# Keys and queries of the last two row blocks as seven products of half matrices, with the mixing drawn into the same block

## The chip, the cores and the metric

The kernel runs on one core of a Trainium2 chip. The metric is the device time of one execution in microseconds (us). Five engines work side by side, each on its own list of instructions in order: TensorE (PE) multiplies matrices into banks of PSUM, VectorE (DVE) and ScalarE (ACT) work element by element and can read PSUM, GpSimd (POOL) does small work and issues transfers that add to their target, and SyncE (SP) issues all other transfers (DMA).

## The reference

`x` has 2048 rows of 512 numbers. Everything is float32.

```python
xn = _layernorm(x)
# A: linear attention, 32 heads of 16
q, k, v = heads(xn2 @ wqkv)                # xn2: xn, 512 x 1536 weights
phi = lambda t: jnp.where(t > 0, t + 1, jnp.exp(t)) + 1e-6
kv = einsum("bhsd,bhse->bhde", phi(k), v); z = phi(k) summed over rows
s = ((phi(q) @ kv) / (phi(q) . z + 1e-6)) @ wo
# B: mixer
h = gelu(_layernorm(xn) @ w1)              # 512 x 512
hs = (four column groups of h, shifted by +1, -1, +2, -2 rows) @ w2
x1 = xn + hs
g = silu(x1 + gelu(_layernorm(x1) @ w3) @ w4)   # 512 x 1376 x 512
return x + s * g
```

Here `xn2` is `xn` (the block A is called with it), and `heads` cuts the columns into q, k and v.

## The kernel before, in words

**Precision.** TensorE multiplies in the rounded type float32r. Each operand is cut into a high and a low part (`rounded`, L478: ACT copies to float32r, DVE subtracts), and each product is three matmuls: high by high, high by low, low by high (`products`, L470). A product over 512 columns of weights with the four chunks of 128 that make up 512 is 12 matmuls of 128x512.

**Work.** The 16 row tiles of 128 rows form four blocks of four (block b holds tiles 4b to 4b+3). `XT` is x turned, loaded by `load_u` (L635); its parts are `UT`, with two columns at either side for the shifts (`split_halo`, L658). Per tile, `key` (L752) and `query` (L765) each run 12 matmuls against `WK` or `WQ`. The mean of a row is taken out afterwards: DVE computes `ps - mean * (column sums of the weights)` in one operation, on `wneg` and `qneg` (`feature_k`, L739, and `query`). Then ACT makes relu and exp, scaled by the row's inverse deviation `rs1`. The key's feature goes to `gram` (L776), 12 matmuls that gather features times normalized rows in the four PSUM banks `acc`; its sum over rows is gathered by an adding transfer on POOL (`zacc`). The query's feature goes to memory (`pqd`, by SP and, adding, by POOL).

`mixer` (L873) multiplies by `W1` (48 matmuls of 512 columns per block, `mix1`), applies the gelu, and makes the forms for the product with `W2`. That product is done by seven products of half matrices in place of eight (`seven`, L783: Winograd's form; the sums of quarters are `s1` to `s4` on one side and `t1` to `t4` on the other, `right`, L806). `mix2(i)` (L882) runs it for tiles i and i+2, in 42 matmuls of 256 columns; three PSUM banks (`pa`, `pb`, `pe`) are used in turn, and ACT and DVE take partial results out between products. An adding transfer puts the normalized rows to it. Half-way, the gathered matrix is multiplied by `wv` and `wo` (`kv`, `m`).

The second half runs block after block over W3 and W4 (`up_pair`, `down`, again by sevens) and the attention's product (`attend_pair`), and ends with `gate`. `make_pair` (L942) loads and cuts a pair of columns of W3; `AHEAD` (L425) says how many microseconds ahead of need its buffers may be taken.

**Order.** The functions only add operations to a plan. `Plan.emit` (L267) then simulates the engines at build time with fixed costs and puts the operations in order: PE's follow the order in which they were added, except that later ones may go ahead inside a window of 12 us; each other operation has a due time, worked back from the matmul that needs it (`deadlines`, `backward`). SBUF is a fixed number of buffers (`counts`, L431: 90 pieces "p" of 516 numbers per partition); a buffer is handed out no earlier than `lead` microseconds ahead of the due time. `SOONER` (L1401) is a table of operation numbers and quarter microseconds by which their due time is moved. PSUM is handed out as four banks "acc" and four "mm".

The order around the change is written in the loop over b = 1, 2, 3 behind the opening: it loads block b and runs its keys and queries between pieces of earlier blocks' mixing: blocks 0 and 1 are mixed in the pass for block 2, block 2 in the pass for block 3, and the last block behind the loop.

Of the kernel before, what the change touches and what calls it, by code (L numbers as in the profile page):

```python
# [12 lines left out]
AX = mybir.AxisListType  # L13

P = 128
EPS = 1e-5
DEN_EPS = 1e-6
TINY = 1e-6
# [67 lines left out]
class Plan:  # L86
# [180 lines left out]
    def emit(self, first, lead, reserve, window, ahead, table=()):  # L267
# [20 lines left out]
        while left:  # L288
# [105 lines left out]
def linear_attn_gated_by_mixer(  # L394
# [20 lines left out]
    QT = 4  # L415
# [18 lines left out]
    for tag, n in counts.items():  # L434
# [62 lines left out]
    arow = memory("arow", S + 2 * EDGE, 1)  # L497

    def pool(busy, reads, out, fn):
        pl.add("POOL", busy, busy, reads, [out], fn)  # L500
# [112 lines left out]

    ABC = {}

    def spread_a(b):

        ps = pl.new("mm", f"ab{b}", F32, 512)[:QT, :P]
        pl.transpose(ps, au[:, b * QT:(b + 1) * QT], ident.all)
        t = pl.new("p", f"ar{b}", F32, PIECE)[:QT, :P]  # L620
        pl.act(t, ps, AF.Copy)
        row = arow[:, EDGE + b * BT:EDGE + (b + 1) * BT]
        pl.store(row.via(lambda ap: ap.rearrange("o (j p) -> (o j) p", p=P)), t)

    def join_a(b):

# [8 lines left out]
    def load_u(b, parts):  # L635

        n = BT // parts
        UT[b] = [[pl.new("p", f"u{b}_{c}{k}", F32R, PIECE) for k in "hl"] for c in range(NC)]
        for q in range(parts):
            o = q * n  # L640
            for c in range(NC):
                if q == 0:
                    XT[b, c] = piece(f"xt{b}_{c}")
                if c and parts > 1:
                    if q == 0:
                        pl.load(XT[b, c], xt[b, c])
# [3 lines left out]
                pl.load(src, xt[b, c][:, o:o + n])  # L650
                hi, lo = (t[:, 2 + o:2 + o + n] for t in UT[b][c])
                if b == q == 0 and parts > 1:
                    pl.ts(hi, src, 1.0, None, ALU.mult)
                    split(lo, src, hi)
                else:
                    rounded(hi, lo, src)

    def split_halo(b):  # L658
        for c in range(NC):
# [102 lines left out]

    pqd = {i: memory(f"pqd{i}") for i in range(NT)}

    def query(i):  # L765
        ps = bank(f"q{i}")
        project(ps, i, WQ, range(NC))
        t, e, r = (piece(f"q{n}{i}") for n in "ter")
        pl.stt(t, qneg, mean(mv1, i), ps, ALU.mult, ALU.add)
# [4 lines left out]
        pl.soon(pl.gather(pqd[i].all, e))  # L774

    def gram(i):  # L776
        xh, xl, kh, kl = GK.pop(i)
# [437 lines left out]
    WQ = Weights("wq", wqkv[0])  # L1215
    WQ.split()
    sums(WQ, bank("qsum"), qneg)
    query(0)
    gram(0)
    query(1)  # L1220
    load_u(1, 1)
    load_rows(QT)
    scale_x(QT, 1)
    gram(1)
    query(2)
    gram(2)
    query(3)
    gram(3)
    key(QT)
    pl.load(hal.all, halo.rearrange("p q c -> p (q c)"))  # L1230
    scale_u(0)
    spread_a(0)
    W1 = Weights("w1", w1)
    early_s, early_f = EARLY
    fill = [lambda f=f: make_w4(f) for f in early_f] + [lambda s=s: make_pair(s) for s in early_s]
    for b in range(1, NQ):
        t0 = b * QT

        def more(n):
            if b > 1:  # L1240
                for _ in range(n):
                    if fill:
                        fill.pop(0)()

        for j in range(b == 1, QT):
            load_rows(t0 + j)
        split_halo(b - 1)
        scale_x(t0 + (b == 1), QT - (b == 1))
        scale_u(b)
        if b == 2:  # L1250
            pl.early = 20.0
            prepare_w2()
            pl.early = 0.0
            mixer(0)
        if b > 1:
            load_u(b, 1)
            key(t0)
        if b == 2:
            mix2(0)
        query(t0)  # L1260
        if b == 2:
            mix2(1)
        spread_a(b)
        more(2)
        if b > 1:
            mixer(b - 1)
        key(t0 + 1)
        query(t0 + 1)
        more(2)
        gram(t0)  # L1270
        key(t0 + 2)
        if b > 1:
            mix2(t0 - QT)
        else:
            W1.center(by_dma=True)
            W1.split()
        query(t0 + 2)
        more(2)
        gram(t0 + 1)
        key(t0 + 3)  # L1280
        if b > 1:
            mix2(t0 - QT + 1)
        query(t0 + 3)
        more(2)
        if b < NQ - 1:
            gram(t0 + 2)
            gram(t0 + 3)


    b = NQ - 1  # L1290
    split_halo(b)
    mixer(b)
    gram(NT - 2)
    gram(NT - 1)
# [39 lines left out]
    for b in range(NQ):  # L1334
# [64 lines left out]
                gate(b * QT + QT - 1, a, o, D // 2, late=True, by_dma=False, whole=o > 0)  # L1399

    SOONER = (  # L1401
# [6 lines left out]
    )  # L1408
    pl.emit(first=6.0, lead={"p": 14.0, "w": 14.0, "ab": 10.0}, reserve={"p": 20, "w": 1, "ab": 0}, window=12.0,
            ahead=6.0, table=SOONER)  # L1410
# [37 lines left out]
```

## Time and profile before

| | us |
|---|---|
| median of 3 runs | 519.35 (519.34 to 519.38) |
| span of the profiled execution | 517.6 |
| busy PE, DVE, ACT, POOL in it | 511.2, 394.0, 324.8, 102.8 |

The span runs from the first instruction to the last; the run's time has 1.7 us more around it. In a profile, an engine's busy share is the union of its instructions; matmuls overlap, so what one of them costs in a stream is the distance of two starts and not its duration. "L146" is a line of the kernel, mostly a helper's, so groups are told apart by the tiles that they write (`k`, `q`, `g`, `h`, `pb`).

### The profile page before, as it was taken

Reading aid. Unit: us, or ns where it says so; the run is one execution under the profiler, and the core shown is the slowest. Engines: PE = TensorE matmul, PEld = TensorE weight load, DVE = VectorE, ACT = ScalarE, POOL = GpSimd, SP = SyncE. Lnnn points to the kernel's source line nnn. Section 1 sums busy time; section 2 is a strip of 40 time slices with the busy share of each in tenths; the row PEclk is TensorE's granted clock in tenths of the full one; section 3 lists DMA queues with packets and bytes.
Section 4 is the critical chain, followed back from the end, with each engine's and each line's share of the span. In section 5 each row is a group of like instructions: output and inputs, shape, how many; then the busy total and the mean of one; then the engine's idle time right before and its main releaser. Section 6 shows DMA issues by size and latency. Waiting matters only on the chain.

```text
span 517.6 us, 8927 instructions
## 1 busy us (share of the span) xinstructions
PE 511.2 (99%) x3005; PEld 445.0 (86%) x3005; DVE 394.0 (76%) x788; ACT 324.8 (63%) x664; POOL 102.8 (20%) x195
## 2 busy tenths in 40 slices
PE   8999999999999999999999999999999999999996
PEld 6777888988888888898889989899898898999985
DVE  5884987569567838999999999655886657895635
ACT  5899784579558657787866755345453545535621
POOL 1378643431363022211100001000020000200000
PEclk9999999999999999999999999999999999999999
DMA  8759994375976389989767759648488376687604
GB/s 277 255 101 248 225 205 97 74 172 182 220 169 162 68 185 249 259 261 262 287 200 225 237 175 249 212 152 208 133 214 276 122 201 157 179 248 225 243 1 122
DMA packets 73281, 100.12 MB, mean 193 GB/s; under 512 B 7844, under 2 KB 30900, under 8 KB 73236
## 3 DMA queue, kind: packets, MB, share of 16 engines
q1 hardware_dynamic: 63876, 82.52, 50.6%
q0 software_dynamic: 9360, 17.04, 19.9%
q8 instruction: 23, 0.38, 0.3%
q14 instruction: 22, 0.18, 0.1%
HBM read 60.33 MB, written 30.81 MB: 176 GB/s over the span
## 4 chain that ended last, share of the span: by engine, by line
PE 91%; ACT 5%; DVE 2%; DMA 1%; issue 1%; SPq 0%; DVEq 0%
PE acc L146 22%; PE pb L146 10%; PE k L146 8%; PE h L146 8%; PE q L146 7%; PE g L146 7%; PE pe L146 5%; PE pbs L146 5%; PE pbm L146 4%; PE pa L146 3%; PE pes L146 2%; PE a L146 2%; PE pem L146 2%; PE pas L146 1%; ACT y L167 1%; PE pam L146 1%
## 5 line engine op out<-in xcount | busy, mean ns | idle before, releaser
L223 POOL DMA_DIRECT2D th<-in_x x14 | 12.2, 919 | 247.3 <-PE a L146 126.2
L167 ACT ACTIVATE p<-pb 128x256 f32<-128x256 f32 x20 | 7.7, 385 | 25.8 <-PE pb L146 25.4
L223 POOL DMA_DIRECT2D o<-x x16 | 15.0, 935 | 40.4 <-DVE o L189 19.7
L223 POOL DMA_DIRECT2D zacc<-kr x16 | 14.6, 910 | 41.8 <-DVE kr L199 33.6
L167 ACT ACTIVATE th<-xo 128x512 f32<-128x512 f32 (+1 forms) x16 | 9.7, 619 | 19.3 <-DVE xo L189 16.2
L167 ACT ACTIVATE gf<-gf 128x512 f32<-128x512 f32 (+1 forms) x40 | 20.9, 523 | 0.8
L223 POOL DMA_DIRECT2D pqd<-qe x16 | 14.7, 921 | 28.9 <-ACT p5m L167 10.0
L167 ACT ACTIVATE p<-pe 128x256 f32<-128x256 f32 x20 | 7.7, 386 | 18.9 <-PE pe L146 18.9
L189 DVE TENSOR_TENSOR xo<-acc,xo 128x512 f32<-128x512 f32 (+1 forms) x16 | 10.3, 670 | 11.4 <-PE acc L146 11.4
L199 DVE SCALAR_TENSOR_TENSOR kt<-wneg,mv,k 128x512 f32<-128x512 f32 x16 | 11.9, 742 | 9.4 <-PE k L146 8.5
L199 DVE SCALAR_TENSOR_TENSOR kr<-kt,kr 128x512 f32<-128x512 f32 x16 | 11.0, 690 | 10.4 <-ACT kt L167 10.4
L199 DVE SCALAR_TENSOR_TENSOR qt<-qneg,mv,q 128x512 f32<-128x512 f32 x16 | 11.9, 742 | 7.2 <-PE q L146 7.1
L167 ACT ACTIVATE ht<-ht 128x512 f32<-128x512 f32 x16 | 10.0, 630 | 11.5 <-DVE ht L189 11.4
L189 DVE TENSOR_TENSOR gf<-u,pe 128x256 f32<-128x256 f32 x20 | 8.3, 416 | 11.2 <-PE pe L146 11.2
L189 DVE TENSOR_TENSOR gf<-pa,p 128x256 f32<-128x256 f32 x20 | 8.4, 418 | 10.5 <-PE pa L146 10.4
L189 DVE TENSOR_TENSOR ht<-h,abc 128x512 f32<-128x512 f32 x16 | 10.8, 686 | 6.5 <-PE h L146 6.5
L167 ACT ACTIVATE x<-x,nm,rs 128x512 f32<-128x512 f32 x16 | 12.5, 802 | 2.9 <-POOL nm L189 2.9
L167 ACT ACTIVATE qr<-qt,rs 128x512 f32<-128x512 f32 x16 | 11.4, 715 | 4.1 <-DVE qt L199 4.1
L590 DVE BATCH_NORM_STATS2 st<-o 128x6 f32<-128x512 f32 x16 | 10.9, 683 | 1.8 <-DMA o<-x 1.8
L167 ACT ACTIVATE kr<-kt,rs 128x512 f32<-128x512 f32 x16 | 11.4, 715 | 1.2 <-DVE kt L199 1.1
L167 ACT ACTIVATE y<-o,nm,rs 128x512 f32<-128x512 f32 x16 | 12.0, 805 | 0.1
L167 ACT ACTIVATE kt<-kt,rs 128x512 f32<-128x512 f32 x16 | 11.4, 715 | 0.1
(1559 smaller groups left out, 2195.9 us busy)
## 6 DMA issues: line engine op xcount, KB each, us to landing
w_s<-in_w SPq DMA_DIRECT2D x28, 256.0 KB, 5.5
x<-in_x SPq DMA_DIRECT2D x16, 256.0 KB, 5.2
zacc<-kr POOLq DMA_DIRECT2D x16, 256.0 KB, 3.9
pqd<-qr SPq DMA_DIRECT2D x16, 256.0 KB, 3.3
pqd<-qe POOLq DMA_DIRECT2D x16, 256.0 KB, 5.4
o<-x POOLq DMA_DIRECT2D x16, 256.0 KB, 4.6
x1d<-o SPq DMA_DIRECT2D x16, 256.0 KB, 4.9
pq<-pqd SPq DMA_DIRECT2D x16, 256.0 KB, 6.0
```

The source lines that it names most:

```text
L146: lambda: nc.tensor.matmul(out.get(), lhs.get(), rhs.get(), start=start, stop=stop, skip_group_check=more))
L167: nc.scalar.activation(out.get(), src.get(), func, scale=get(scale), **kw)
L189: self.vec(eng, out, [a, b], lambda: self.e(eng).tensor_tensor(out.get(), a.get(), b.get(), op=op), True)
L199: lambda: self.nc.vector.scalar_tensor_tensor(out.get(), a.get(), get(s), b.get(), op0=op0, op1=op1),
L223: lambda: self.nc.gpsimd.dma_start(out.get(), get(src), accum_op=ALU.add), mb=mb)
L590: pl.add("DVE", .62, .69, [xv], [st], lambda: nc.vector.bn_stats(st.get(), xv.get()))
```

## The change

In blocks 2 and 3, keys and queries of a pair of tiles (i, i+2) come from one product by sevens: the turned rows are the left matrix, with its halves by rows (tiles 0, 1 against 2, 3 of the block) and by chunks (0, 1 against 2, 3), and the right matrix is [WK | WQ], with its halves by chunks and by weight. A product is 2 chunks x 3 matmuls of 512 columns. Keys and queries of tile i come out as `p1` and `u2`, those of tile i+2 as `pb` (left in PSUM) and `p5`.

For this the rows must be centred before they are multiplied: the means are turned into a row in memory (`spread_m`), spread over all partitions by a transfer, and subtracted from `XT` by DVE (`make_u`), which also makes the four sums of quarters (on POOL) and their parts. The correction by `wneg` and `qneg` falls away in these blocks. The forms of the two weights are made once (`forms_kq`). The rows of x of blocks 2 and 3 are loaded twice, once for their moments (`stats_of`) and later for the gram. The parts of `W1` are stored to memory after they are made and loaded again for blocks 2 and 3 (`w1_for`).

The loop gives way to a written order, in which the mixing of block 0 stands among the keys of block 1, that of block 1 behind them and before the keys of block 2, and those of blocks 2 and 3 among and behind the keys of their own block. The number of pieces goes from 90 to 96, `AHEAD` is longer, a buffer's lead is cut when few are free (`SCARCE`), the table `SOONER` is a new one, and the descriptor scratch of POOL's transfers is set to 4096 bytes. Blocks 0 and 1 keep their form (`KQ1 = False`).

```diff
+SCARCE = 3.0
...
                             n = lead[t.tag] * (1.5 if len(q) > reserve[t.tag] else 1)
+                            if t.tag == "p":
+                                n = min(n, SCARCE * (len(q) - need + 1))
...
+    SUMS = "POOL"
+    SOON = {"T": 24.0, "u": 5.0}
-    AHEAD = 30.0, 20.0, 10.0, 0.0, 0.0
+    AHEAD = 70.0, 50.0, 30.0, 10.0, 0.0
...
-    counts = {"w": 2, "p": 90, "h": 6, "sm": 12, "ab": 2, "acc": 4, "mm": 4}
+    counts = {"w": 2, "p": 96, "h": 6, "sm": 10, "ab": 2, "acc": 4, "mm": 4}
...
+    def make_u(b):
+        m = piece(f"um{b}")
+        pl.fetch(m, mrow[:, b * BT:(b + 1) * BT].via(lambda ap: ap.to_broadcast([P, BT])))
+        for c in range(NC):
+            pl.tt(XT[b, c], XT[b, c], m, ALU.subtract)
+            rounded(*(t[:, 2:2 + BT] for t in UT[b][c]), XT[b, c])
...
+        for n, u, v, op in ((0, q[1, 0], q[1, 1], ALU.add), (1, parts[0], q[0, 0], ALU.subtract),
+                            (2, q[0, 0], q[1, 0], ALU.subtract), (3, q[0, 1], parts[1], ALU.subtract)):
+            for c in range(2):
+                pl.tt(parts[n][c], u[c], v[c], op, eng=SUMS)
+            hl = rounds(f"us{b}_{n}")
+            rounded(*hl, s[n])
...
-    def feature_k(i, ps):
+    def feature_k(i, ps, centred=False):
         t, r = piece(f"kt{i}"), piece(f"kr{i}")
-        pl.stt(t, wneg, mean(mv1, i), ps, ALU.mult, ALU.add)
-        pl.act(r, t, AF.Relu, scale=col(rs1, i))
-        pl.act(t, t, AF.Exp, scale=col(rs1, i))
+        if not centred:
+            pl.stt(t, wneg, mean(mv1, i), ps, ALU.mult, ALU.add)
+            ps = t
+        pl.act(r, ps, AF.Relu, scale=col(rs1, i))
+        pl.act(t, ps, AF.Exp, scale=col(rs1, i))
...
+    def keys_queries(b, j):
+        i, k = b * QT + j, b * QT + j + 2
...
+        go(pb, "a11", "b11")
+        pl.act(p1, pb, AF.Copy)
+        go(pe, "s1", "t1")
+        pl.act(p5, pe, AF.Copy)
+        go(pb, "s2", "t2", False)
+        pl.act(u2, pb, AF.Copy)
+        go(pa, "a12", "b21")
+        pl.tt(p1, pa, p1, ALU.add)
+        go(pb, "s3", "t3", False)
+        pl.tt(p5, pb, p5, ALU.add)
+        go(pe, "s4", "b22", False)
+        pl.tt(u2, u2, pe, ALU.add)
+        feature_k(i, p1, True)
+        go(pb, "a22", "t4", False)
+        feature_k(k, pb, True)
+        feature_q(i, u2)
+        feature_q(k, p5)
...
+        ORD = [("q", 4), ("w1", 0), ("k", 5), ("g", 4), ("q", 5), ("st", 2), ("k", 6), ("g", 5), ("mix", 0), ("q", 6), ("w2",), ("k", 7), ("g", 6), ("T",), ("q", 7), ("g", 7)]
+    ORD += [("a", 2), ("h", 1), ("m2", 0), ("mix", 1), ("m2", 1), ("u", 2), ("m2", 4), ("m2", 5), ("x", 2),
+           ("kq", 2, 0), ("st", 3), ("g", 8), ("w1", 2), ("h", 2), ("a", 3), ("mix", 2), ("g", 10), ("kq", 2, 1), ("m2", 8), ("g", 9),
+           ("u", 3), ("m2", 9), ("g", 11), ("x", 3),
+           ("kq", 3, 0), ("g", 12), ("w1", 3), ("kq", 3, 1), ("g", 14)]
...
-    nc = bacc.Bacc("TRN2", target_bir_lowering=False, num_devices=1)
+    nc = bacc.Bacc("TRN2", target_bir_lowering=False, num_devices=1, dynamic_dma_scratch_size=4096)
```

In the written order "q", "k", "kq" and "g" are queries, keys, both by sevens and grams; "mix" and "m2" the two products of the mixing; "st", "x" and "u" the first load of the rows with their moments, the second load with the scaling, and `make_u`; "w1", "w2" and "T" the forms of W1, of W2 and of the two weights; "a" and "h" the row scales and the halo.

More of the change, by code (lines that the diff above doesn't have):

```diff
@@ L614, in linear_attn_gated_by_mixer, with spread, spread_m @@
     ABC = {}
-    def spread_a(b):
[L618 to L623, printed above, removed]
+    def spread(name, src, b, row):
+        ps = pl.new("mm", f"{name}b{b}", F32, 512)[:QT, :P]
+        pl.transpose(ps, src, ident.all)
+        t = pl.new("p", f"{name}r{b}", F32, PIECE)[:QT, :P]
+        pl.act(t, ps, AF.Copy)
+        pl.store(row.via(lambda ap: ap.rearrange("o (j p) -> (o j) p", p=P)), t)
+    def spread_a(b):
+        spread("a", au[:, b * QT:(b + 1) * QT], b, arow[:, EDGE + b * BT:EDGE + (b + 1) * BT])
+    def spread_m(b):
+        spread("c", means(mv1, b * QT, (b + 1) * QT), b, mrow[:, b * BT:(b + 1) * BT])
     def join_a(b):
@@ L763, in linear_attn_gated_by_mixer, with feature_q @@
     pqd = {i: memory(f"pqd{i}") for i in range(NT)}
[L765 to L769, printed above, removed]
+    def feature_q(i, t):
+        e, r = (piece(f"q{n}{i}") for n in "er")
         pl.act(by_block(e), by_chunk(t), AF.Relu, scale=col(ns1, i))
@@ L774, in query, with forms_kq, go @@
         pl.soon(pl.gather(pqd[i].all, e))
+    def query(i):
+        ps = bank(f"q{i}")
+        project(ps, i, WQ, range(NC))
+        t = piece(f"qt{i}")
+        pl.stt(t, qneg, mean(mv1, i), ps, ALU.mult, ALU.add)
+        feature_q(i, t)
+    TW = {}
+    def forms_kq():
+        k, q = WK.raw, WQ.raw
+        t = [[piece(f"kq{n}_{c}") for c in range(2)] for n in range(4)]
+        for c in range(2):
+            pl.tt(t[0][c], q[c], k[c], ALU.subtract)
+        for c in range(2):
+            pl.tt(t[1][c], q[c + 2], t[0][c], ALU.subtract)
+        for c in range(2):
+            pl.tt(t[2][c], q[c + 2], q[c], ALU.subtract)
+        for c in range(2):
+            pl.tt(t[3][c], k[c + 2], t[1][c], ALU.subtract)
+        for n in range(4):
+            TW[f"t{n + 1}"] = []
+            for c in range(2):
+                hl = rounds(f"kq{n}_{c}")
+                rounded(*hl, t[n][c])
+                TW[f"t{n + 1}"].append(hl)
+        TW["b11"], TW["b21"], TW["b22"] = WK.hl[:2], WK.hl[2:], WQ.hl[2:]
+    def keys_queries(b, j):
+        i, k = b * QT + j, b * QT + j + 2
+        pa, pb, pe = (bank(f"{n}k{i}") for n in ("pa", "pb", "pe"))
+        p1, p5, u2 = (piece(f"{n}k{i}") for n in ("p1", "p5", "u2"))
+        def go(ps, x, y, start=True):
+            products(ps, [both(U[b][x][c], j * P, (j + 1) * P) + TW[y][c] for c in range(2)], start, more=not start)
+        go(pb, "a11", "b11")
[15 more added lines that the diff above has]
+        feature_q(k, p5)
     def gram(i):
@@ L1221, in linear_attn_gated_by_mixer @@
     load_u(1, 1)
-    load_rows(QT)
-    scale_x(QT, 1)
+    if KQ1:
+        forms_kq()
+    scaled(1)
     gram(1)
+    if KQ1:
+        stats_of(1, False)
     query(2)
@@ L1227, in linear_attn_gated_by_mixer @@
     query(3)
+    if KQ1:
+        make_u(1)
     gram(3)
-    key(QT)
     pl.load(hal.all, halo.rearrange("p q c -> p (q c)"))
@@ L1232, in linear_attn_gated_by_mixer @@
     spread_a(0)
+    split_halo(0)
+    if not KQ1:
+        plain_u(1)
+        key(4)
+        scale_u(1)
+    spread_a(1)
     W1 = Weights("w1", w1)
@@ L1235, in linear_attn_gated_by_mixer @@
     fill = [lambda f=f: make_w4(f) for f in early_f] + [lambda s=s: make_pair(s) for s in early_s]
[L1236 to L1287, printed above, removed]
+    if KQ1:
+        ORD = [("kq", 1, 0), ("w1", 0), ("st", 2), ("g", 4), ("kq", 1, 1), ("g", 6), ("g", 5), ("mix", 0), ("w2",), ("g", 7)]
+    else:
+        ORD = [("q", 4), ("w1", 0), ("k", 5), ("g", 4), ("q", 5), ("st", 2), ("k", 6), ("g", 5), ("mix", 0), ("q", 6), ("w2",), ("k", 7), ("g", 6), ("T",), ("q", 7), ("g", 7)]
+    ORD += [("a", 2), ("h", 1), ("m2", 0), ("mix", 1), ("m2", 1), ("u", 2), ("m2", 4), ("m2", 5), ("x", 2),
[3 rows of a table added]
+    DO = {"x": scaled, "kq": keys_queries, "w1": w1_for, "st": stats_of, "g": gram, "mix": mixer, "w2": prepare_w2,
+          "a": spread_a, "h": split_halo, "m2": mix2, "u": make_u, "k": key, "q": query, "T": forms_kq}
+    for what, *args in ORD:
+        pl.early = SOON.get(what, 0.0)
+        DO[what](*args)
+    pl.early = 0.0
+    t0 = NT - QT
     b = NQ - 1
@@ L1292, in linear_attn_gated_by_mixer @@
     mixer(b)
-    gram(NT - 2)
-    gram(NT - 1)
+    gram(13)
+    gram(15)
     WV, WO = Weights("wv", wqkv[2]), Weights("wo", wo)
```

53 lines of the change are left out of this document (52 added, 1 removed), and 6 rows, old and new, of the table SOONER.

## The prediction

> **What bounds the kernel now.** I read the head of the page first: busy shares, then the 40 slices.
>
> ```profile
> span 517.6 us, 8927 instructions
> PE 511.2 (99%) x3005; PEld 445.0 (86%) x3005; DVE 394.0 (76%) x788; ACT 324.8 (63%) x664; POOL 102.8 (20%) x195
> ...
> PE   8999999999999999999999999999999999999996
> ...
> DVE  5884987569567838999999999655886657895635
> ...
> q1 hardware_dynamic: 63876, 82.52, 50.6%
> ```
>
> TensorE (PE) is at 9 in every slice but the first and the last. Busy matmul time is modelled, so a high share need not mean that nothing waits. The waits of PE and the chain of waits settle that.
>
> ```profile
> PE warm L146 <- POOL ones L503: 1.1, 1, 1.1
> PE k L146 <- DMA wk_s<-in_wqkv: 0.4, 1, 0.4
> PE pem L146 <- ACT p5m L167: 0.3, 1, 0.3
> ```
>
> ```profile
> PE 91%; ACT 5%; DVE 2%; DMA 1%; issue 1%; SPq 0%; DVEq 0%
> ```
>
> ```profile
> 42.60 2.78 PE k L146 x12
> 45.38 0.11 PE ab L151
> 45.49 2.77 PE q L146 x12
> 48.27 0.11 PE ab L151
> 48.37 2.77 PE k L146 x12
> ```
>
> PE names only three waits, 1.8 us together, and two of them belong to the opening. The chain is PE for 91%, and piece follows piece without a hole: a key of 12 matmuls of 512 columns starts at 42.60, and the transposition behind it at 45.38. So the time is the sum of what PE has to stream, and a matmul of 512 columns costs 2.78 / 12 = 0.232 us in it (not the longer duration of a single one, which overlaps its neighbours).
>
> The other engines matter by stage. The windows below cut block 1's keys and queries (30 to 76), the first mixing with the start of block 2 (76 to 116), the rest of blocks 2 and 3 (116 to 224), and the opening of the second half (224 to 320). Columns: stretch, length, busy PE, PEld, DVE, ACT, POOL with counts, clock, DMA share, GB/s.
>
> ```profile
> 30.00:76.00 46.00, 45.98 (x199) 36.73 (x199) 35.35 (x60) 41.20 (x72) 31.77 (x65) 1.00 0.91 209
> 76.00:116.00 40.00, 40.00 (x214) 34.06 (x213) 25.93 (x58) 24.63 (x45) 13.87 (x29) 1.00 0.53 122
> 116.00:158.00 42.00, 42.00 (x223) 35.55 (x222) 29.47 (x61) 29.31 (x52) 16.47 (x35) 1.00 0.73 181
> 158.00:202.00 44.00, 44.00 (x233) 37.36 (x231) 31.05 (x61) 31.13 (x57) 9.99 (x13) 1.00 0.69 165
> 202.00:224.00 22.00, 21.72 (x114) 18.24 (x112) 19.17 (x41) 18.69 (x37) 2.73 (x6) 1.00 1.01 254
> 224.00:320.00 96.00, 95.93 (x650) 87.10 (x649) 94.84 (x197) 66.13 (x150) 9.68 (x12) 1.00 0.78 232
> ```
>
> The change works in blocks 2 and 3. There, over 108 us, VectorE (DVE) is busy 29.47 + 31.05 + 19.17 = 79.7 us, ScalarE (ACT) 79.1 us, and the DMA engines 0.73 x 42 + 0.69 x 44 + 1.01 x 22 = 83.2 us. All three have about a quarter free. From 224 to 320 DVE has nothing free (94.84 of 96), so work pushed past 224 would be paid in full.
>
> **What goes from PE.** Before, a pair of row tiles (i, i+2) costs a key and a query for each tile: 4 groups of 12 matmuls, 48. After, seven products of two half chunks with three roundings each: 7 x 2 x 3 = 42, all of 512 columns. Blocks 2 and 3 have four pairs, so 4 x 6 = 24 matmuls go: 24 x 0.232 = **5.56 us off PE**. The means as a row need two more transpositions of the kind at 45.38, 2 x 0.11 = 0.22 us. Grams, mixing and the whole second half keep their matmuls; block 1 keeps the old form, as the switch for it is off.
>
> **What the side engines get.** The prices are these.
>
> ```profile
> L199 DVE SCALAR_TENSOR_TENSOR qt<-qneg,mv,q 128x512 f32<-128x512 f32 x16 | 11.9, 742 | 7.2 <-PE q L146 7.1
> L189 DVE TENSOR_TENSOR ht<-h,abc 128x512 f32<-128x512 f32 x16 | 10.8, 686 | 6.5 <-PE h L146 6.5
> L189 DVE TENSOR_TENSOR w_s0l<-w_sf,w_s0h 128x512 fp32r<-128x512 f32 x5 | 3.4, 685 | 0.2 <-ACT w_s0h L167 0.2
> ```
>
> ```profile
> L167 ACT ACTIVATE w_s0h<-w_sf 128x512 fp32r<-128x512 f32 x5 | 3.2, 634 | 0.5 <-DVE w_sf L189 0.4
> L167 ACT ACTIVATE gs<-g 128x512 f32<-128x512 f32 x4 | 2.4, 589 | 0.0
> ```
>
> DVE loses the mean correction of 8 keys and 8 queries: 16 x 0.742 = 11.9 us. It gains, per block, 4 centrings and 4 low parts of the sums, and per pair 3 additions out of PSUM: 16 + 12 = 28 operations of about 0.686, 19.2 us; and once the weights' forms, 8 differences and 8 low parts, 11.0 us. Net +18.3 us, of which 7.3 must lie in blocks 2 and 3 and 11.0 may lie in block 1. ACT gains 12 copies out of PSUM at 0.589, and 8 + 8 roundings at 0.634: 7.1 + 10.1 = 17.2 us. In blocks 2 and 3 that leaves DVE at 87.0, ACT at about 91 of the 102.7 us (108 - 5.34) that PE then needs. Both fit, so I cost them at nothing; the cover is PE's own stream, and where it is gone every microsecond counts in full, as from 224 on.
>
> POOL gains 16 sums of 128x256, an operation that this trace does not show. From below stands the memset without any input, from above the four-column power:
>
> ```profile
> L596 POOL TENSOR_TENSOR rs<-w,nhalf 128x4 f32<-128x4 f32 (+3 forms) x11 | 10.5, 954 | 0.9
> ...
> L509 POOL MEMSET zacc<- 128x512 f32 x1 | 0.5, 525 | 0.0
> L504 POOL MEMSET ident<- 128x128 f32 x1 | 0.2, 206 | 0.0
> ```
>
> Between 0.21 and 0.95 us; I take 0.53, the memset that touches as many numbers as a sum reads. Eight in a row are 4.2 us per block (1.7 to 7.6). Behind them on POOL queue the transfers of row sums and mixed rows and the scales of the rows; none of these is due within that time.
>
> ```profile
> 92.02 0.72 PE pem L146 x6
> ```
>
> A half-width matmul takes 0.72 / 6 = 0.12 us. In the written order the sums stand ahead of two second mixings of the block before (2 x 42 x 0.12 = 10.1 us) in block 2, and of one with a gram (5.0 + 12 x 0.232 = 7.8 us) in block 3. PE has that to do while POOL adds. Hidden.
>
> The mixing that moves into its own block takes its instructions with it, the broadcast of the row scales on SP's queue and the 16 residual transfers on POOL's among them; their number stays, and they come some tens of microseconds earlier, before the opening of the second half needs SP and DVE for W3.
>
> DMA gains 8 stores and 16 loads of W1's halves, 8 second loads of rows of x and 2 rows of means spread over the partitions: 34 x 0.262 MB = 8.9 MB on the queue of SP. That queue took 50.6% of 517.6 = 261.9 us for 82.52 MB, so 3.17 us per MB: 28 us of engine time. The 8 stores fall between 76 and 116 at a share of 0.53; 26 transfers, 6.8 MB, 21.6 us, fall in blocks 2 and 3. SP issues them in the planner's order, with the stores of queries and of mixed rows behind them; who waits for those needs them tens of microseconds later. I take nothing, and the end where they don't fit is a rival. The smaller scratch meets POOL's own transfers:
>
> ```profile
> pqd<-qe POOLq DMA_DIRECT2D x16, 256.0 KB, 5.4
> ```
>
> Should fewer than now be in flight, the second of two waits up to 5.4 us. What they carry (row sums, query features, the first residual) is read much later: nothing to that on PE's path. What the freed 12 KB buys, six more buffers, feeds the earlier loads of W3 and is costed at nothing too.
>
> New waits inside the products: one bank gathers four of the seven products in turn, and each time a copy or an addition must leave it first. Between two uses stands at least one other product, 6 x 0.232 = 1.39 us, against 0.59 or 0.69 for the eviction. In the second mixing the same pattern runs with products half as long, and all of it cost 0.3 us of named wait (the row of pem above). Bounds: nothing, to 0.6 us for each of 12 evictions that finds another operation ahead of it, 7.2 us. I take 0.5. The last bank of a pair is now read by two activations directly, of about the duration of
>
> ```profile
> L167 ACT ACTIVATE kr<-kt,rs 128x512 f32<-128x512 f32 x16 | 11.4, 715 | 1.2 <-DVE kt L199 1.1
> ```
>
> that is 1.43 us, while PE goes on with a gram of 2.8 us in banks of its own.
>
> The table of due times is new, and the rows that ordered the first loads by force are gone. The first product waits for wk_s (0.4 us above); the loads' natural order by due time puts the same tiles first. I take nothing, within 0.7 either way.
>
> **The sum:** 519.35 - 5.56 + 0.22 + 0.5 = **514.5 us**. The profiled span of 517.6 lies 1.7 below the median; what surrounds the span does not change, so the new span should be about 512.8.
>
> **Rivals.** (1) **DMA fills blocks 2 and 3.** 83.2 + 21.6 = 104.8 us of engine time stand against 102.7: over by 2.1, and if the earlier loads of three W3 pairs (6 x 0.262 x 3.17 = 5.0 us) come in before 224 as well, by 7.1. Time 516.6 to 521.6, if a share of 1 can't be passed. For it: the sum. Against it: 30 to 76 ran at 0.91 with PE busy 45.98 of 46.00, and 202 to 224 at 1.01 and 254 GB/s. Chance 0.16.
>
> (2) **Evictions hold PE** in the new products: 12 waits of 0.2, half an eviction's slip, add 2.4: 516.9. For it: DVE and ACT both rise to 85 to 89% there. Against: the one wait of 0.3 in half-length products. Chance 0.12.
>
> (3) **DVE takes PE's place, and it is slower.** The place is blocks 2 and 3. If the weights' forms are not made before 116, DVE has 87.0 + 11.0 = 98.0 of 102.7 us. If each POOL sum then keeps DVE waiting for its whole length, at 0.954 that is 15.3 more, 113.3: 10.6 over, 525.1 us. It ends above 520.4 from (102.7 + 5.9 - 98.0) / 16 = 0.66 us per sum on. For it, that POOL and DVE do meet: a two-element copy on POOL takes 0.51 at one time and 0.18 at another.
>
> ```profile
> 146.79 0.51 POOL L665 CAST u_2h<-hal 128x2 fp32r<-128x2 f32 x1
> 147.39 0.19 POOL L666 TENSOR_TENSOR u_2l<-hal,u_2h 128x2 fp32r<-128x2 f32 x1
> 147.53 0.18 POOL L665 CAST u_3h<-hal 128x2 fp32r<-128x2 f32 x1
> ```
>
> Against it: there it is POOL that is stretched, and the forms may be made 24 us ahead. Chance 0.14. [...]
>
> **How the numbers follow.** The forecast (513 to 516) has 0.58. A measurement of this kernel can tell about 0.2%, 1.04 us, from no change: faster ends at 518.3, slower begins at 520.4. Rival 2 is faster; rival 1 splits into 0.06 faster, 0.05 same, 0.05 slower; rival 3 is slower. Faster 0.58 + 0.12 + 0.06 = 0.76, same 0.05, slower 0.19. The range runs from 512.9 (no stall, the opening 0.7 better, a little of the old waits gone) to 520.8; above it is most of rival 3 and the end of rival 1.
>
> **What would show it.** Right: 2983 or so matmul records (24 fewer, two transpositions more), no new PE wait above 0.5 us, and mixing ending some 5 us earlier than now, with DVE about 412 us busy in all. Rival 1: DMA share at 1.0 from 116 to 220, and PE waiting for xt, w1 or x loads. Rival 2: PE waits on pa, pb or pe of keys and queries, released by ACT or DVE. Rival 3: DVE above 95% before 220, PE waiting for low parts of the sums or, past 224, for low parts of W3 and W4. An opening that loses time would show as a later start of the first gram:
>
> ```profile
> 22.11 0.40 PE L146 MATMUL g<-k0h,x0h 128*128 128x512 f32 x1
> ```
>
> Two microseconds lost there would make the forecast wrong without any of the rivals.

## The result and the profile after

The changed kernel takes **524.96 us** (median of 4 runs, 523.32 to 525.16) against 519.37 (519.34 to 519.57) for the kernel before: ratio 1.0098, 95% interval 1.0084 to 1.0113. It is slower by 5.6 us; 514.5 was forecast, and the range ended at 520.8.

The page after, its head, the slices of two engines and the granted clock, SP's DMA queue and the chain of waits:

```profile
span 523.2 us, 8982 instructions
PE 511.5 (98%) x2983; PEld 444.3 (85%) x2983; DVE 417.0 (80%) x816; ACT 338.9 (65%) x694; POOL 117.9 (23%) x207
...
PE   8999999998999899999999999999999999999996
...
PEclk9999999998999899999999999999999999999999
...
q1 hardware_dynamic: 68788, 91.44, 54.8%
...
PE 80%; ACT 13%; DVE 3%; issue 2%; DMA 1%; SPq 0%; ACTq 0%; DVEq 0%
```

There are 22 matmul records fewer, as the change says, and yet PE is busy as long as before: busy time is modelled and takes in a slower clock (behind the first wait below, a matmul of 512 columns lasts 0.63 us at a clock of 0.50 and 0.39 at 1.00). PE dips below 9 at two places inside the blocks, in the tenth and the fourteenth slice (118 to 131 and 170 to 183), and the granted clock dips with it. PE's longest waits are new:

```profile
PE pbk L147 <- DVE o L190: 2.1, 1, 2.1
PE pbm L147 <- DVE o L190: 2.0, 1, 2.0
PE warm L147 <- POOL ones L508: 1.0, 1, 1.0
```

Here is the first of them in the order of time, as PE, DVE and POOL record it (start, length, operation; for PE in brackets the wait and who ended it):

```profile
119.08 0.28 PE L147 MATMUL pbm<-w_t2h,hs21l 128*128 128x256 f32 x1
...
121.44 0.50 PE L147 MATMUL pbk<-wk_0h,u_0h 128*128 128x512 f32 x1 [2.07 <-DVE o L190]
```

```profile
116.50 0.41 DVE L190 TENSOR_TENSOR o<-pbm,p5m 128x256 f32<-128x256 f32 x1
116.91 4.14 DVE L190 TENSOR_TENSOR u_0l<-xt,u_0h 128x512 fp32r<-128x512 f32 x1
120.97 0.41 DVE L190 TENSOR_TENSOR o<-pam,p1m 128x256 f32<-128x256 f32 x1
```

```profile
115.08 1.76 POOL L190 TENSOR_TENSOR us<-xt,xt 128x256 f32<-128x256 f32 x2
...
117.27 1.87 POOL L190 TENSOR_TENSOR us<-us,xt 128x256 f32<-128x256 f32 x2
118.67 1.82 POOL L190 TENSOR_TENSOR us<-xt,us 128x256 f32<-128x256 f32 x2
```

One subtraction on DVE, of a kind that took 0.686 before, lasts 4.14 us while POOL adds. Behind it in DVE's queue stands the eviction of the bank pam. PE cannot go on without that bank's place and stands 2.07 us. A second price follows, in the clock. Columns: stretch, length, busy PE, granted clock, DMA share, GB/s.

```profile
119.20:121.40 2.20, 0.16 (x2) 1.00 1.01 227
121.40:123.40 2.00, 1.96 (x9) 0.60 1.00 242
123.40:125.40 2.00, 2.00 (x9) 0.55 1.03 297
125.40:127.40 2.00, 2.00 (x13) 1.00 0.82 154
```

For some four microseconds behind the wait the granted clock averages 0.55 to 0.6: 0.40 x 2.0 + 0.45 x 2.0 = 1.7 us more. The second stop, until 178.82, is put together from several lengthened operations of DVE ahead of the addition that empties pbm:

```profile
172.80 2.43 DVE L190 TENSOR_TENSOR u_2l<-xt,u_2h 128x512 fp32r<-128x512 f32 x1
175.15 1.21 DVE L190 TENSOR_TENSOR u_3l<-xt,u_3h 128x512 fp32r<-128x512 f32 x1
176.29 1.21 DVE L190 TENSOR_TENSOR us_2l<-us,us_2h 128x512 fp32r<-128x512 f32 x1
...
178.36 0.40 DVE L190 TENSOR_TENSOR o<-pbm,p5m 128x256 f32<-128x256 f32 x1
```

4.85 us for three of 0.686 each. The clock behind it is 0.76, 0.50 and 0.89 in three stretches of 2 us. The four sums of each kind on POOL, two chunks in each of two blocks, with least, median and longest time in ns:

```profile
L190 POOL TENSOR_TENSOR us<-xt x4: 747/856/1053, 105.5 to 167.6; 128x256 f32<-128x256 f32 x4
...
L190 POOL TENSOR_TENSOR us<-xt,xt x4: 860/1412/2559, 115.1 to 173.2; 128x256 f32<-128x256 f32 x4
...
L190 POOL TENSOR_TENSOR us<-us,xt x4: 1042/1174/2992, 117.3 to 178.8; 128x256 f32<-128x256 f32 x4
```

**Where the time went, in all.** From the starts of all matmuls one can reckon what PE loses: the distance from one start to the next, less the columns of the first at 0.4525 ns (232 ns for 512). Summed up, in us, up to a point of the span:

```
lost by            40    110    130    170    190    230    end
before            7.7    8.4    8.4    8.8    9.0   11.6   19.9
after             9.1   10.3   14.7   16.4   20.5   21.6   30.6
sums on DVE (e1)  8.6    9.5   11.3   13.0   13.7   16.5   23.7
```

The kernel after loses 10.7 us more than before, and its matmuls want 5.3 less (24 x 0.232, less two transpositions): 5.4, where the spans differ by 523.2 - 517.6 = 5.6. Of the 10.7, the opening has 1.4; the stretches 110 to 130 and 170 to 190, with the two stops, lose 4.4 and 4.2 (before: 0.1 and 0.2).

### The profile page after: what moved, and what is told of

The parts are those of the page before. It is cut to its first block, busy times and chain, and to the rows that moved or that the text cites. A ratio compares the mean times of both kernels' runs of the same rounds, so it can differ in the third digit from the quotient of the medians.

```text
span 523.2 us, 8982 instructions
## 1 busy us (share of the span) xinstructions
PE 511.5 (98%) x2983; PEld 444.3 (85%) x2983; DVE 417.0 (80%) x816; ACT 338.9 (65%) x694; POOL 117.9 (23%) x207
## 3 DMA queue, kind: packets, MB, share of 16 engines
q1 hardware_dynamic: 68788, 91.44, 54.8%
## 4 chain that ended last, share of the span: by engine, by line
PE 80%; ACT 13%; DVE 3%; issue 2%; DMA 1%; SPq 0%; ACTq 0%; DVEq 0%
PE acc L147 23%; PE pb L147 11%; PE h L147 6%; PE pe L147 6%; PE g L147 5%; PE pbs L147 4%; PE k L147 4%; PE pa L147 3%; PE q L147 3%; PE pbm L147 3%; PE pes L147 2%; PE a L147 2%; PE pbk L147 2%; PE pem L147 1%; ACT qe L168 1%
## 5 line engine op out<-in xcount | busy, mean ns | idle before, releaser
L224 POOL DMA_DIRECT2D pqd<-qe x16 | 16.3, 1060 | 23.3 <-ACT ht L168 9.0
L190 DVE TENSOR_TENSOR ht<-h,abc 128x512 f32<-128x512 f32 x16 | 10.7, 682 | 4.1 <-PE h L147 3.9
L200 DVE SCALAR_TENSOR_TENSOR qz<-pq,zb 128x512 f32<-128x512 f32 x16 | 10.8, 685 | 0.7 <-DMA pq<-pqd 0.7
L168 ACT ACTIVATE u<-pb 128x256 f32<-128x256 f32 x20 | 7.7, 383 | 5.5 <-PE pb L147 5.5
L200 DVE SCALAR_TENSOR_TENSOR th<-th,so 128x512 f32<-128x512 f32 (+1 forms) x17 | 10.9, 653 | 0.4
L200 DVE SCALAR_TENSOR_TENSOR pq<-pq,rd 128x512 f32<-128x512 f32 x16 | 11.0, 687 | 0.1
L601 POOL TENSOR_TENSOR rs<-w,nhalf 128x4 f32<-128x4 f32 (+2 forms) x10 | 10.6, 1061 | 0.8
```

Source lines behind the costliest of these rows:

```text
L168: nc.scalar.activation(out.get(), src.get(), func, scale=get(scale), **kw)
L190: self.vec(eng, out, [a, b], lambda: self.e(eng).tensor_tensor(out.get(), a.get(), b.get(), op=op), True)
L200: lambda: self.nc.vector.scalar_tensor_tensor(out.get(), a.get(), get(s), b.get(), op0=op0, op1=op1),
L224: lambda: self.nc.gpsimd.dma_start(out.get(), get(src), accum_op=ALU.add), mb=mb)
L601: lambda: g.tensor_tensor(out.get(), src.get(), nh.get(), op=ALU.pow))
```

## The experiments

The kernel before was measured again beside each group of experiments, at 519.15 to 519.74; ratios are to it. Where nothing else is said, an edit is made to the changed kernel.

**e1: the sums on DVE, order kept.** The plan still counts them to POOL, so every instruction stands where it stood, but DVE issues them.

```diff
-                pl.tt(parts[n][c], u[c], v[c], op, eng=SUMS)
+                def add(o=parts[n][c], p=u[c], q=v[c], op=op):
+                    nc.vector.tensor_tensor(o.get(), p.get(), q.get(), op=op)
+                pl.vec("POOL", parts[n][c], [u[c], v[c]], add, True)
```

> Changed kernel with its 16 sums of quarters issued on DVE at the very places in the order where POOL had them; every other engine's list is the same. Theory A (a POOL sum that reads SBUF and a DVE operation with two SBUF inputs exclude each other, so a low part of 4.14 us stood in front of an eviction): the low parts of the turned rows take 0.68 us, the two PE waits of 2.1 and 2.0 us on DVE o go, with them the slowed matmuls behind (about 2 us each): 525.0 - 8 = 517 us, give or take 1. Theory B (DVE is simply full from 80 to 121, 40.3 of 41.0 us): DVE gets 16 x 0.34 = 5.4 us more work, the two waits grow by about 2.7 each: 527 or more. Theory C (the waits come from late transfers): unchanged, 525.

Measured: 518.39 us, ratio 0.9982 (0.9969 to 0.9994). The sums, the same subtraction with the eviction of pam behind it, the stretch 80 to 121 (columns: busy PE, PEld, DVE, ACT, POOL, clock, DMA share, GB/s), and PE's waits for DVE:

```profile
L689 DVE TENSOR_TENSOR us<-xt x4: 392/418/420, 107.7 to 164.8; 128x256 f32<-128x256 f32 x4
```

```profile
116.75 0.66 DVE L190 TENSOR_TENSOR u_0l<-xt,u_0h 128x512 fp32r<-128x512 f32 x1
117.33 0.42 DVE L190 TENSOR_TENSOR o<-pam,p1m 128x256 f32<-128x256 f32 x1
```

```profile
80.00:121.00 41.00, 40.62 (x253) 35.90 (x252) 40.67 (x91) 30.79 (x60) 8.99 (x13) 1.00 0.77 202
```

```profile
PE pbm L147 <- DVE o L190: 0.5, 2, 0.3
PE pbk L147 <- DVE u_1l L190: 0.3, 1, 0.3
```

After has this for the same stretch:

```profile
80.00:121.00 41.00, 39.20 (x240) 34.39 (x238) 40.33 (x77) 31.50 (x62) 14.42 (x21) 1.00 0.76 202
```

DVE has more work here, is as full (40.67 of 41 against 40.33), and PE does not stop: 13 matmuls more are done by 121. So a full DVE is not the cause; the sums' place on POOL is. It costs 524.96 - 518.39 = **6.6 us**, about what the two stops with their clock are worth (8.6 by the table, less the 2.5 that e1 loses there: 6.1).

**e2: the sums left out, a memset on POOL in their places** (the products then read zeros).

> Leaves the sums of quarters out: POOL writes zeros into the same tiles at the same places and reads nothing. Theory A (what blocks is POOL's reading of SBUF): DVE's low parts go back to 0.68 us, no PE wait over 0.5 us between 100 and 200 us, 517 us, give or take 1. If any POOL write blocks DVE: low parts of 1 us and more remain, the time lies between 518 and 523. Theory B (DVE is full): DVE's work is the same as in the changed kernel, 525.

Measured: 515.93 us, 0.9944 (0.9927 to 0.9961).

```profile
L689 POOL MEMSET us<- x16: 308/647/1493, 105.2 to 177.8; 128x256 f32 x16
```

POOL is occupied at the same moments, if more briefly (0.65 us in the median), DVE's subtractions of 128x512 for the same tiles take 0.66 to 0.69, and no stop comes. So the stop comes with sums that read SBUF (4.14 us) and not with memsets that read nothing (0.69 at most): POOL's occupation alone does not bring it. DVE's 16 sums cost e1 about 2.5 us against this.

**e8: the sums planned for DVE as well** (`SUMS = "DVE"`, with the same due times).

> The changed kernel with the sums of quarters assigned to DVE in the plan itself (SUMS), so that the planner knows of them. [...]

Measured: 518.71 us, 0.9984 (0.9972 to 0.9996), the same as e1. Planning for it wins nothing here.

**e7 and e11: the disputed operations by themselves.** Two small programs that compute nothing of the reference (they store zeros): DVE and POOL working side by side, and in e7 matmuls behind pauses of rising length.

> Not the computation: it measures the disputed costs by themselves and stores zeros. Stages of ten DVE operations of 128x512 and eight POOL operations of 128x256, alone and together; then 56 matmuls of 512 columns, four times after a PE pause of 1 to 6 DVE operations. Theory A: with POOL sums beside, DVE operations with two SBUF inputs take longer (ten of them 6 us alone, 6 + 8 x 0.9 = 13 us beside eight sums), and with one SBUF input and one from PSUM or with POOL memsets they don't. Theory B: DVE's ten take 6 us in every stage. For the pause: if a wait of about 2 us costs as much again in slower matmuls behind, matmuls behind pauses of 2 us and over start at 0.43 us apart for some 2 to 4 us, and at 0.22 or 0.23 behind pauses of about 1 us.

Ten DVE operations each: alone; beside eight sums on POOL; beside eight memsets; with one input in PSUM beside sums; with a single input beside sums (a fence each, in this order). Then POOL's sums beside DVE and alone (least, median, longest ns).

```profile
L54 DVE TENSOR_TENSOR donly<-a,b x10: 691/692/695, 4.2 to 10.8; 128x512 f32<-128x512 f32 x10
```

```profile
L54 DVE TENSOR_TENSOR dsum<-a,b x10: 683/1095/1257, 18.5 to 28.4; 128x512 f32<-128x512 f32 x10
```

```profile
L54 DVE TENSOR_TENSOR dset<-a,b x10: 683/692/694, 29.1 to 35.6; 128x512 f32<-128x512 f32 x10
```

```profile
L57 DVE TENSOR_TENSOR dfix<-fix,b x10: 683/691/691, 36.3 to 42.9; 128x512 f32<-128x512 f32 x10
```

```profile
L60 DVE BATCH_NORM_STATS2 dstat<-a x10: 685/694/697, 43.5 to 50.1; 128x6 f32<-128x512 f32 x10
```

```profile
L63 POOL TENSOR_TENSOR psum<-c,d x8: 733/1051/1052, 19.2 to 26.8; 128x256 f32<-128x256 f32 x8
```

```profile
L63 POOL TENSOR_TENSOR pnone<-c,d x8: 732/736/741, 11.8 to 17.5; 128x256 f32<-128x256 f32 x8
```

Of the DVE operations tried, only those with two inputs in SBUF were stretched beside POOL's sums, and both sides were: 0.692 to 1.095, and 0.736 to 1.051. With one input in PSUM, or a single one, DVE took 0.691 and 0.694. The sum on POOL takes 0.736 alone; the prediction took 0.53 within 0.21 to 0.95. Ten operations (7.2 us alone) and eight sums (6.4 alone) took 10.6 us together (from the first start to the end of the last, 18.5 to 29.1), where one behind the other they would take 13.6: by their recorded lengths, whole instructions did not exclude each other.

The pauses (in brackets) and what the clock did behind each:

```profile
68.92 14.86 PE L85 MATMUL ps<-br,w 128*128 128x512 f32 x56 [1.77 <-DVE w L83]
```

```profile
68.90:72.40 3.50, 3.48 (x10) 0.67 0.00 0
72.40:76.00 3.60, 3.60 (x15) 0.85 0.00 0
76.00:83.50 7.50, 7.50 (x34) 1.00 0.00 0
```

56 matmuls take 56 x 0.232 = 13.0 us at full clock; behind a pause of 1.77 us they took 14.86. So a stop of this length alone, with nothing else at work, can bring the slow clock; the last section has a stop that did not.

> Not the computation: it stores zeros. Eight DVE subtractions of 128x512 from SBUF, each behind a single-source operation, beside twelve POOL sums in a row: plain, with a rounded result, with chained sums, with both engines on the same tiles, and with every third POOL operation an adding transfer. In the changed kernel one such subtraction took 4.14 us, as long as four sums. If DVE loses its turn to several sums in one of these patterns, its longest subtraction is 2 us or more in that stage; if it only ever waits for the sum at work, none is over 1.5 us in any, and the 4.14 us stay unexplained in their length.

Measured: of five arrangements the longest DVE subtraction came in the one with adding transfers on POOL's queue, as in the kernel:

```profile
L60 DVE TENSOR_TENSOR dmoved<-a,b x8: 666/669/1528, 59.6 to 69.6; 128x512 f32<-128x512 f32 x8
```

None comes near 4.14. In the other four no subtraction took over 0.96 us (0.67 to 0.68 in the median), while POOL's sums took 1.08 to 1.12 in the median (0.736 alone, in e7): there almost only POOL was held up. That each can hold up the other is shown (DVE to 1.095 in e7, POOL to 1.12 here); which one it is, and why one DVE operation was held through several sums running, is not.

**e4: the kernel before with a descriptor scratch of 4 KB.**

> The kernel before with nothing changed but the descriptor scratch of 4096 bytes. If the smaller scratch costs nothing, as the prediction had it: 519.4, within 0.5. If it holds POOL's transfers back: POOL's issues and landings get longer (5.4 us for the query's before) and the time rises by a microsecond or more.

Measured: 519.31 us, 1.0002 (0.9992 to 1.0013). The transfers that it concerns:

```profile
pqd<-qe POOLq DMA_DIRECT2D x16, 256.0 KB, 5.5
```

5.5 us to landing against 5.4: the smaller scratch costs nothing. This kernel also had one stop of 1.08 us, at 484.71, and the clock stayed at 1.00 behind it.

**e3, e6, e9: the opening.** e3 puts the 27 rows back that ordered the first loads (those of the old table for operations up to number 186, in place of the new table's five); e6 is e3 with the sums on DVE; e9 takes the order of the first 36 us from a plan with those rows, and behind it keeps e1's.

> The changed kernel with the rows of the old table for the opening's loads and first operations (numbers up to 186) in place of the new ones; the planner puts later operations in another order too. If the opening's loss of about 1.7 us by 40 us comes from the table: PE's lost time by 40 us goes from 9.5 back to 7.8, and with the POOL sums still there the time is 523, give or take 2, with PE waits of 1 to 2 us behind DVE. If the table isn't the cause: 525.

> The kernel with the old table's opening rows, and the sums of quarters issued on DVE in POOL's places. Both remedies add up if they are independent: 518.4 - 1.7 = 516.7, give or take 1. If the opening isn't the table's doing: 518.4.

> The sums on DVE in POOL's places, and the first 36 us in the order that the old table's opening rows give; behind them the order of the run with the sums on DVE is kept, operation by operation. If the opening is worth what PE's lost time by 40 us shows (8.7 us with the new table, 7.6 with the old rows): 518.4 - 1.1 = 517.3, give or take 0.6. If the loss of the opening is only pushed further back: 518.4.

Measured: e3 525.95 us, 1.0134 (1.0116 to 1.0152); e6 519.52, 1.0007 (0.9997 to 1.0017); e9 **517.98**, 0.9974 (0.9964 to 0.9984). In all three PE has lost no more than 7.5 us by 40 (before 7.7): the old rows do bring the opening back. But the other rows act on what comes behind, and a new opening shifts it. In e3 the same stop is longer:

```profile
PE pbm L147 <- DVE o L190: 6.1, 2, 3.5
```

```profile
116.35 4.80 DVE L190 TENSOR_TENSOR u_3l<-xt,u_3h 128x512 fp32r<-128x512 f32 x1
```

e9, which holds the rest in place, is 0.4 us under e1, with intervals that overlap. It is the shortest of the kernels that do all the work, 1.3 us under the kernel before beside it.

**e5, e10, e12, e13, e14: the new written order with plain keys.** e5 keeps the change's buffers, scratch, transfers, table and written order, but makes the keys and queries of blocks 2 and 3 with 12 matmuls each, without centring (and the two rows of means that it needs), sums and forms.

```diff
+    def plain_kq(b, j):
+        i, k = b * QT + j, b * QT + j + 2
+        key(i)
+        key(k)
+        query(i)
+        query(k)
...
-    DO = {"x": scaled, "kq": keys_queries, ...
+    DO = {"x": scaled, "kq": plain_kq, ...
```

e10 is e5 with the opening rows of before; e12 is e5 with W1 kept in its buffers (no 8 stores and 16 loads); e13 is e12 with the rows of x loaded once; e14 is e5 with a shorter lead of the loads (`AHEAD` 30, 20, 10, 0, 0).

> The changed kernel's order, buffers, second loads, W1 reload and scratch, but keys and queries of blocks 2 and 3 by 12 matmuls each as before: no centring, no sums, no forms of the weights. Theory A (the loss hangs on the POOL sums, and the opening loses 1.6 us): 519.4 + 1.6 = 521, give or take 1, with no PE wait of 2 us. Rival (the order or the 33 added transfers make the waits): 524 or more, with PE waits of 1 us and over between 100 and 200.

> Keys and queries by 12 matmuls as before in the changed order (the run without sevens, 523.2), with the old table's opening rows; later operations are put in a new order too. If the opening makes 2.1 of its 3.9 us over the kernel before: 521.1, give or take 1. If the written order with its added transfers makes them: 523.

> As the run without sevens (523.2), but the parts of W1 stay in their buffers: no 8 stores and 16 loads. If transfers in the way make the 3.9 us: about 521 (24 of the 32 added transfers are gone). If not: 523, within 1.

> W1 kept, and the rows of x of blocks 2 and 3 loaded once as before, so no added transfer of 256 KB is left. If transfers make the 3.9 us: 519.5 to 520.5. If the order of the work does: 523, within 1, or more, since four more buffers per block are held for longer.

> The run without sevens with the old AHEAD (30, 20, 10). If the early W3 work crowds blocks 2 and 3: 521 to 522. If it relieves the stage behind: 524 or more, with PE waits past 220. If it does neither: 523.

Measured: e5 523.22 us, 1.0066 (1.0046 to 1.0085); e10 523.01; e12 522.87; e13 523.33; e14 522.60. All lie within 0.8 us, and 2.9 to 4.1 above the runs of before beside them. So neither the opening nor W1's transfers, the second loads or the lead, each taken away by itself, brings that back; what the five share is the written order, the later rows of the table, and the number of buffers and the way they are handed out (`counts`, `SCARCE`, `SOON`). The last were not tried apart.

**e15, e16, e17, e18: order or fitted rows.** A row of the table names one operation by its number and moves its due time. The table of before has 37 later rows, written for that program; the change brings 11 of its own (the expectations, which say 39 and 12, miscount). e15 is the kernel before with its opening rows alone, e16 is e10 and e17 is e6 without the later rows.

```diff
-        176, 10, 179, 58, 181, 172, 183, 184, 186, 161, 241, 4, 245, 24, 247, 6, ... 4489, 34, 4590, 4,
+        176, 10, 179, 58, 181, 172, 183, 184, 186, 161,
```

> The kernel before, with its table of due times cut behind row 186: the opening stays ordered as it was, and the 39 later rows, each of which moves one numbered operation's due time, are gone. Nothing else differs. Theory F (fit): those rows were fitted to this program; a program with other numbers loses what they bring, and that is the 3.9 us by which the plain keys in the new written order are slower. Then this kernel takes 522 to 524. Theory O (order): the written order of the work makes the 3.9; then this kernel stays at 519.4, within 0.8. Between, 520.2 to 522, each has a part.

> Plain keys and queries in the new written order with the opening rows of before (523.01 with the 12 later rows of the change), now without those later rows, which name operations by number and so meet other operations here than in the change. Theory F: the foreign rows do little, 522 to 524, about as much as the kernel before without its rows. Theory O: the same, 522 to 524, but 3 or more above the kernel before without its rows. Theory H (harm): the foreign rows are what costs; then 519 to 521.

> The change with its sums on DVE and the opening rows of before (519.52 with the 12 later rows), now without the later rows: what the sevens give where neither program has fitted rows. Against the kernel before without its rows it should be 4.8 to 5.3 faster by theory F (24 matmuls fewer, nothing else different in kind): 517.5 to 519.5 if that one takes 522 to 524. By theory O it is 518 to 521 and the kernel before without its rows is at 519.4, so no gain of that size shows.

Measured: e15 520.73 us, 1.0025 (1.0014 to 1.0035); e16 522.54, 1.0065 (1.0053 to 1.0078); e17 529.60, 1.0189 (1.0174 to 1.0204). Each theory has a part: the rows of before are worth 1.4 us, the written order with plain keys, and the buffers and transfers that come with it, cost 1.8, and the change's rows bring plain keys nothing (523.01 with them, 522.54 without). For the sevens they do much: without them e17 is 10.1 us slower than e6. The expectation for e17 missed by 9 to 12, and the reason is a single stop:

```profile
PE pbk L147 <- DVE ht L190: 7.1, 1, 7.1
```

```profile
155.24 2.49 DVE L190 TENSOR_TENSOR ht<-h,abc 128x512 f32<-128x512 f32 x4 [4.07 <-DMA abc<-arow]
```

DVE stands 4.07 us on the broadcast row scales abc, at a DMA share of 1.07 to 1.10 from 148 to 154; behind ht in its queue stands what PE needs; behind the stop the clock is at 0.50 until 162 (7.1 us, and half of the 6 us from 156 to 162, are the 10.1). Just ahead of it DVE had stood 3.46 us for the high part of x of tile 11, since ACT waited for the second load of these rows (2.68 us on in_x): a load, too, was late there, but abc landed last. With the mixing in its own block, abc is made and wanted within one block. e10 and e16 have waits of 5.0 and 5.4 us for it on DVE; e1 and the kernel after have none.

e18 is e16 with the broadcasts' due times 10 us earlier.

```diff
         pl.fetch(t.all, arow[:, a:a + BT + W].via(lambda ap: ap.to_broadcast([P, BT + W])))
+        if b > 0:
+            JOINS.extend((len(pl.ops) - 1, 40))
...
-            ahead=6.0, table=SOONER)
+            ahead=6.0, table=SOONER + tuple(JOINS))
```

> Plain keys in the new written order with neither program's later rows (522.54), and the broadcasts of the row scales (abc) of blocks 1, 2 and 3 given a due time 10 us earlier, so that SP's queue issues them ahead of the transfers that stood before them. Nothing else is changed by hand. In the 522.54 kernel VectorE stood 5.4 and 3.4 us on abc ahead of the first scaling of a mixing. Theory S (scales): the mixing, moved into its own block, gets its row scales late, VectorE's work piles up behind, and that is the 1.8 us against the kernel before without its rows (520.73); then this takes 520.5 to 521.3. Theory N: VectorE had nothing else to do in that time, the late scales cost only the 0.7 us of named wait or nothing; then 521.8 to 522.6.

Measured: 522.54 us, 1.0051 (1.0032 to 1.0071), no change. Block 1's wait of 3.4 us for abc is gone and DVE stands there for PE instead (3.2); block 2's, of 5.0, remains. So for block 1 theory S falls; for block 2 it was not tried, since the wait did not go. Where these 1.8 us lie, and whether the order or the buffers cost them, stays open.

## Why the prediction was wrong, step by step

- **"Hidden" is the step that failed**: sixteen sums on POOL at nothing, because PE has work in that time. PE had, but DVE's subtractions with two inputs in SBUF did not keep their 0.69 us beside the sums (4.14 for one, 4.85 for three). The sums' price was within the bounds (0.736 alone); who pays it was looked for on POOL's queue, and it is paid on DVE, in front of an eviction. This is the 6.6 us between e1 and after, and more than the 5.6 us by which the change is slower.
- **Rival 3 named the mechanism, and 525.1 us, but not the way.** It filled DVE by 16 full lengths. No run shows a sum that keeps DVE waiting for its whole length each time: in e7 ten subtractions and eight sums took 10.6 us, not 13.6, and in the kernel after one subtraction took 4.14 us, as long as four sums. DVE is as full in e1 without a stop, so a total did not decide; one operation of 4.14 us and three of 4.85 together did, in front of an eviction, and the clock added nearly as much again (1.7 us behind the first 2.07). So that its 525.1 meets the measured 524.96 is luck. "There it is POOL that is stretched" held for two-element operations; at full size both sides were in e7 (0.692 to 1.095, 0.736 to 1.051), and almost only POOL in four parts of e11 (1.08 to 1.12, DVE 0.67 to 0.68).
- **PE's 5.56 less held**, in records (2983, as forecast). e1 shows how little of it arrives: 518.39, 0.8 us under the 519.15 beside it, while 5.3 left PE. The table says where the rest is: e1 loses 0.9 us more than before by 40 and 3.6 more between 110 and 190 (4.2 against 0.6), and the later stretches give 0.9 back.
- **"I take 0.5" for the evictions was too small**, if those losses are its own: rival 2 held 2.4 for them. Named waits cover only 0.8 of them in e1 (pbm and pbk), so this part is argued and not shown.
- **"The loads' natural order by due time ... I take nothing" failed in both halves.** The opening lost 1.4 us; e9 lost 1.2 us less than e1 by 40 (7.4 against 8.6), and only 0.4 of it, hardly clear of noise, was left in the end. And the table was not only the opening: its later rows are worth 1.4 us to the kernel before (e15) and 10.1 to the sevens (e17 against e6).
- **The mixing that moves, at nothing:** with plain keys the new order, with its buffers and transfers, costs 1.8 us (e16 against e15). In e17 the row scales come late and PE stands 7.1 us; with the change's rows this does not happen. The step named the broadcast and SP's queue, and did not ask how long ahead of its use it now is.
- **DMA and scratch at nothing held.** SP's queue moved 8.92 MB more (91.44 against 82.52), and no PE wait after the opening is released by a load in the kernel after; rival 1 shows itself in e17 alone. e4 shows the scratch free (ratio 1.0002). DVE at 417.0 (412 forecast), ACT +14.1 (+17.2 forecast): near.

## What to carry to other kernels

POOL, with 77% free, was not free here: beside its sums from SBUF a subtraction of 0.69 us on DVE took 4.14, and DVE had nothing to spare there (busy 40.33 of 41 us). So before work goes to POOL, look at which DVE operations with two SBUF inputs stand beside it, and what stands behind those in DVE's queue. Price a stop of PE of some two microseconds at up to about twice its length, for the clock (1.7 us more behind 2.07 here, 1.9 behind the 1.77 of e7). And where an order was fitted row by row to one program, charge a new program with the loss of that fit first, and keep the rest of the order still when one part is tried (e1, e9), or the trial measures the new order instead.

## What the runs showed of the hardware

- A DVE operation of 0.69 us lasted 4.14 (after) and 4.80 us (e3) beside sums on POOL, where side by side in small programs it lasted 1.1 (e7, median), 1.53 at most (e11). What holds it for so long is open.
- The granted clock fell to 0.50 behind pauses of PE of 1.77 and 2.49 (e7), 2.04 and 2.07 us (after), and not behind one of 1.08 (e4), nor behind the second stop of e3, which lasted 2.62 us (175.82 to 178.44). In the kernel after it stayed there for 3.41 us both times (121.81 to 125.22, 179.83 to 183.24).
- Two of these stops, one with the slow clock behind it and one without. Columns: stretch, length, busy PE, granted clock, DMA share, GB/s; first the kernel after, then e3.

```profile
118.40:121.81 3.41, 1.34 (x11) 1.00 0.99 220
121.81:125.22 3.41, 3.41 (x16) 0.50 1.06 269
```

```profile
173.87:177.28 3.41, 1.95 (x13) 1.00 1.14 245
177.28:180.69 3.41, 2.25 (x13) 1.00 1.06 327
```

The longer idle time, 2.62 us against 2.07, is the one without the fall. What separates the two was not shown.
